# Plain float32 products for the first four steps of a fused attention and feed-forward kernel, with their operands split later

## The chip, the cores and the metric

The kernel runs on one core of one Trainium2 chip. The metric is the device time of one execution in microseconds (us), as the median of several runs. The core has five engines that run their own queues in order and wait for each other through semaphores: TensorE (PE, matrix products; PEld is its weight load), VectorE (DVE), ScalarE (ACT), GpSimd (POOL) and SyncE (SP, which issues the DMAs).

## The reference

```python
s_l = concat([scale * q_l @ k_g.T, where(|i-j| <= 32, scale * q_l @ k_l.T, -1e9)])   # per head
out_l = softmax(s_l) @ concat([v_g, v_l])        # 4 batches, 8 heads, 512 local rows, D = 64
out_g = softmax(scale * q_g @ concat([k_g, k_l]).T) @ concat([v_g, v_l])      # 32 global rows
x = concat([out_g, out_l])                       # 2176 tokens x 512
h = x @ w_in                                     # 512 -> 2048
y = where(h > 0, h, exp(min(h, 0)) - 1) @ w_out  # 2048 -> 512
yn = y / sqrt(mean(y * y) + 1e-6) * rms_g
out = (silu(yn @ w_gate) * (yn @ w_val)) @ w_o2  # 512 -> 1536 -> 512
```

The weights arrive as 64-bit floating-point numbers, and the kernel turns them into float32 on the chip.

## The kernel before

Local attention is done in 16 units (4 batches of 512 rows, 4 units of 128 rows each): `a_S` makes the scores on PE, `a_E` takes the maxima (DVE) and the exponentials (ACT), `a_T` transposes them (PE, copied by ACT), `a_PV` multiplies with V, and `a_N` divides by the sums (DVE) and writes x. The four units of the first batch are done in a start-up stretch. After it come four blocks of 16 steps (`moe_block`), one block for each batch. Step j of a block is `mm1` (12 products of 128x512 for one 128-column slice of the hidden layer), the activation `elu_a` (ACT and DVE), and `mm2` (12 products) of the step before, in two halves; in blocks 0 to 2 the attention units of the next batch stand between these (unit 4 with steps 0 to 2, unit 5 with steps 4 to 6, and so on; scores ahead of the first half of `mm2`, transposes between the halves).

Every operand of a product is kept in two parts, a rounded part of type fp32r and the remainder, and each product is three passes of these parts (`PASSES`, so 3 x 4 = 12 for each `mm1` and `mm2`). The parts are made by an ACT copy and a DVE subtraction: `split_hi` and `split_lo` for weights (L96, L99), `act1` for the activations (`g`, L139 and L140), `a_X` for x (`xT`, L289 and L290).

The weights of the first layer pair come in 16 pieces of 128x1024 (`order1`: two pieces of `w_in`, two of `w_out`, and again). Piece i is loaded as raw 64-bit words (L75), decoded by one ACT operation (L83) and four DVE operations (L90 to L93, `dec_bits`), and split (ACT L96, DVE L99). Pieces 0 to 2 are decoded and split in the start-up; in block 0 step j ends with `w1_decode` of piece j + 3, so that piece 15 goes with step 12. From step 13 on, `w2_task` decodes pieces of the second layer pair. Products of step j need the pieces of group j // 4: steps 0 to 3 use pieces 0 to 3 alone.

PE's order is written out by hand for the whole program, that of DVE and ACT for the start-up alone; elsewhere a scheduler at build time sets a fixed order for each queue, and each engine takes its queue in that order. Lines of the profile are those of this listing:

Of the kernel before, what the change touches and what calls it, by code (L numbers as in the profile page):

```python
# [21 lines left out]
P = 128  # L22
# [20 lines left out]
def fused_kernel(ctx: ExitStack, tc: tile.TileContext, kq, vl, gkq, gv, w_in, w_out, w_gate, w_val, w_o2, rms_g, consts, out):  # L43
# [44 lines left out]
    def dec_bits(x, raw):  # L88
        word = words(raw)
        nc.vector.tensor_scalar(out=x, in0=x, scalar1=HI_MIN, scalar2=HI_MAX, op0=ALU.max, op1=ALU.min)  # L90
# [28 lines left out]
    def elu_a(h, n):  # L119
# [4 lines left out]
        return e  # L124

# [60 lines left out]
    with ExitStack() as ls:  # L186
# [51 lines left out]
        def a_E(u):  # L238
# [30 lines left out]
        def a_N(u):  # L269
# [6 lines left out]
            for par in range(2):  # L276
                o = os_[par]
                nc.vector.tensor_scalar(out=st[:, par, :, 0:1], in0=o[:, :, 64:65], scalar1=1e-9, scalar2=None, op0=ALU.add)
                nc.vector.reciprocal(st[:, par, :, 1:2], st[:, par, :, 0:1])
                nc.vector.tensor_tensor(out=x[:, par], in0=o[:, :, 0:64], in1=st[:, par, :, 1:2].to_broadcast([P, 4, 64]), op=ALU.mult)  # L280

        def a_X(b, cs, xT, pools):

            for c in cs:
                pool, tag = pools[c]
                pt = pool.tile([P, 512], F32, tag=tag, name="xtp")
                for T in range(4):
                    nc.tensor.transpose(pt[:, T * P:(T + 1) * P], x_t[b][:, T, c * P:(c + 1) * P], ident)
                hi = nc.scalar.copy(xT[c][:, 0, :], pt)  # L289
                lo = nc.vector.tensor_tensor(out=xT[c][:, 1, :], in0=pt, in1=f(xT[c][:, 0, :]), op=ALU.subtract)  # L290
            return hi, lo
# [28 lines left out]
        def moe_block(b, slot, after=None):  # L320
            n, t0 = 512, b * 512
            xT, ys, prev = xT_t.pop(b), None, None
            for j in range(16):
                h = mm1(xT, j, n)
# [11 lines left out]
                if carry:  # L336
                    finish_block((2, 3))
                elif prev is not None:
# [15 lines left out]
        raws, n_raw, n_dec = {}, [0], [0]  # L354
# [14 lines left out]
        def w1_bits(i):  # L369
            dec_bits(dxs[i], raws.pop(i))  # L370

        def w1_hi(i):
# [7 lines left out]
            split_hi(dst, dxs[i])  # L380
            dsts[i] = dst

# [17 lines left out]
        with tc.manual_schedule(engines={mybir.EngineType.DVE, mybir.EngineType.Activation}):  # L400
# [10 lines left out]
            w1_abs(0)  # L411
            a_S(0, ATT2)
# [100 lines left out]
        def slot0(j, part, h):  # L513
            g = act1(h, 512, elu_a) if part == 0 else None
# [568 lines left out]
```

## Time and profile before

| | us |
|---|---|
| median of 3 runs (899.45 to 902.01) | 899.69 |
| the profiled execution | 899.1 |
| its span | 897.3 |
| PE busy in it | 864.9 (96%) |
| DVE busy in it | 588.0 (66%) |
| ACT busy in it | 475.8 (53%) |

The span runs from the first to the last instruction; 1.8 us of the profiled execution lie outside it. An engine's busy share is a mean over the whole span; a stretch of it can have another limit than the rest. In the rows, "idle" in brackets is time in which the engine did nothing just before a group, and behind the arrow stands what ended it. Starts are in us from the beginning of the span.

### The profile page before, as it was taken

The page shows a single profiled execution, that of the slowest core. Times are in us where ns is not written, and L with a number is a line of the kernel's source. Part 1 is how long each engine was busy: PE and PEld are TensorE (multiplying, and loading weights), DVE is VectorE, ACT ScalarE, POOL GpSimd, SP SyncE. Part 2 cuts the span into 40 slices and gives each one's busy share as a digit, 9 for nine tenths or more (in the row PEclk, how much of TensorE's full clock was granted, in tenths as well). Part 3 has the DMA queues.
Part 4 walks back from the last instruction along what each step waited for, and adds up shares of the span by engine and source line. Part 5 has one row for each costly group of instructions (what it writes and reads, how often), then busy time and mean ns, then how long its engine had stood idle before and what let it go on. Part 6 is the DMA issues. An engine that isn't in the chain of part 4 may idle for free.

```text
span 897.3 us, 16243 instructions
## 1 busy us (share of the span) xinstructions
PE 864.9 (96%) x6652; PEld 736.4 (82%) x6652; DVE 588.0 (66%) x983; ACT 475.8 (53%) x863; POOL 19.4 (2%) x22
## 2 busy tenths in 40 slices
PE   4789999999999999999999999999999999999997
PEld 3567877888888888677888899997999998899995
DVE  4899988777677764443488656885355776365642
ACT  4677664555564444333456655664455665355531
POOL 0000000000000000000110101000100000000000
PEclk8999999999999999999999999999999999999999
DMA  9786365966678742441405532233222232133200
GB/s 361 289 305 198 124 255 178 300 229 203 228 273 267 248 163 112 148 177 60 167 1 188 179 114 91 96 120 118 81 96 94 95 119 80 59 118 118 95 24 35
DMA packets 60225, 139.26 MB, mean 155 GB/s; under 512 B 4856, under 2 KB 30584, under 8 KB 57592
## 3 DMA queue, kind: packets, MB, share of 16 engines
q1 hardware_dynamic: 60152, 138.23, 44.7%
q8 instruction: 52, 0.85, 0.4%
q14 instruction: 21, 0.17, 0.1%
HBM read 115.15 MB, written 23.07 MB: 154 GB/s over the span
## 4 chain that ended last, share of the span: by engine, by line
PE 79%; DVE 11%; DMA 4%; ACT 3%; issue 1%; SPq 0%; POOL 0%; ACTq 0%
PE y L146 16%; PE A L739 15%; PE h L132 15%; PE o L745 15%; PE Q L739 11%; DMA kq<-in_kq 2%; DVE dx L93 2%; DVE dx L92 1%; PE s L234 1%; PE ptp L252 1%; DVE wA L99 1%; PE o L265 1%; PE hg L675 1%; DMA raw<-in_moe_w_out 1%; DVE dx L90 1%
## 5 line engine op out<-in xcount | busy, mean ns | idle before, releaser
L146 PE MATMUL y<-g,wA 128*128 128x512 f32 x768 | 197.3, 400 | 4.7 <-DVE g L140 4.1
L132 PE MATMUL h<-xT,wA 128*128 128x512 f32 x768 | 186.5, 391 | 1.7 <-DVE xT L290 1.7
L146 PEld LDWEIGHTS y<-g,wA 128*128 128x128 f32 x768 | 140.0, 189 | 40.2 <-DVE g L140 6.0
L132 PEld LDWEIGHTS h<-xT,wA 128*128 128x128 f32 x768 | 143.5, 188 | 32.7 <-DVE xT L290 2.4
L739 PE MATMUL A<-xc,wS 128*128 128x384 f32 (+1 forms) x864 | 155.9, 328 | 1.7 <-ACT t L931 0.9
L739 PEld LDWEIGHTS A<-xc,wS 128*128 128x128 f32 x864 | 145.0, 188 | 6.6 <-ACT t L931 1.3
L745 PE MATMUL o<-wB,p 128*128 128x512 f32 x612 | 147.3, 392 | 0.7 <-DVE p L750 0.3
L745 PEld LDWEIGHTS o<-wB,p 128*128 128x128 f32 x612 | 113.6, 188 | 24.7 <-DVE p L750 2.5
L739 PE MATMUL Q<-xc,wS 128*128 128x384 f32 (+1 forms) x648 | 115.3, 326 | 0.0
L739 PEld LDWEIGHTS Q<-xc,wS 128*128 128x128 f32 x648 | 107.8, 188 | 0.0
L595 DVE TENSOR_TENSOR wS<-wraw,wS 128x1024 fp32r<-128x1024 f32 x63 | 78.5, 1246 | 36.2 <-ACT wS L594 36.0
L754 DVE TENSOR_TENSOR t<-t,Q 128x384 f32<-128x384 f32 (+1 forms) x108 | 55.9, 528 | 37.2 <-PE Q L739 24.0
L594 ACT CAST wS<-wraw 128x1024 fp32r<-128x1024 f32 x63 | 65.9, 1050 | 19.6 <-PE Q L739 11.4
L121 ACT ACTIVATE e<-h 128x512 f32<-128x512 f32 x48 | 29.0, 605 | 69.8 <-PE h L132 69.7
L139 ACT CAST g<-e 128x512 fp32r<-128x512 f32 x64 | 39.8, 621 | 47.3 <-DVE e L123 30.8
L123 DVE SCALAR_TENSOR_TENSOR e<-e,h 128x512 f32<-128x512 f32 x48 | 32.5, 678 | 33.3 <-ACT e L122 33.3
L140 DVE TENSOR_TENSOR g<-e,g 128x512 fp32r<-128x512 f32 x64 | 43.8, 684 | 9.4 <-ACT g L139 9.1
L750 DVE TENSOR_TENSOR p<-p,p 128x384 fp32r<-128x384 f32 x36 | 20.0, 557 | 43.1 <-ACT p L749 43.1
L83 ACT ACTIVATE dx<-raw 128x1024 f32<-128x1024 f32 x34 | 39.2, 1157 | 15.9 <-DMA raw<-in_moe_w_gate 6.0
L90 DVE TENSOR_SCALAR dx<-dx 128x1024 f32<-128x1024 f32 x34 | 23.2, 688 | 33.7 <-ACT dx L83 33.7
L246 ACT ACTIVATE E<-s,mx 128x128 f32<-128x128 f32 x128 | 34.8, 385 | 17.2 <-DVE mx L244 17.2
L92 DVE SCALAR_TENSOR_TENSOR dx<-raw,dx 128x1024 int32<-128x1024 int32 x34 | 41.9, 1239 | 0.6
(173 smaller groups left out, 867.1 us busy)
## 6 DMA issues: line engine op xcount, KB each, us to landing
wraw<-wS SPq DMA_DIRECT2D x63, 512.0 KB, 3.2
raw<-in_moe_w_out SPq DMA_DIRECT2D x14, 1024.0 KB, 7.6
raw<-in_moe_w_in SPq DMA_DIRECT2D x8, 1024.0 KB, 6.0
raw<-in_moe_w_gate SPq DMA_DIRECT2D x6, 1024.0 KB, 6.6
raw<-in_moe_w_val SPq DMA_DIRECT2D x6, 1024.0 KB, 5.7
wS<-raw SPq DMA_DIRECT2D x48, 128.0 KB, 2.4
gvr<-in_gv SPq DMA_DIRECT2D x8, 640.0 KB, 4.7
wS<-dx SPq DMA_DIRECT2D x36, 128.0 KB, 2.1
```

Of the source, the lines that this page charges most:

```text
L83: ins = nc.scalar.activation(x, f(words(raw)[:, :, 1]), AF.Abs)
L92: nc.vector.scalar_tensor_tensor(out=i32(x), in0=word[:, :, 1], scalar=-0x40000000, in1=i32(x), op0=ALU.bitwise_and, op1=ALU.bitwise_or)
L132: nc.tensor.matmul(h[:, :n], W1[c, G][:, ws, o:o + P], xT[c][:, xs, :n], start=(k == 0), stop=(k == 11))
L139: nc.scalar.copy(g[:, 0, :n], e[:, :n])
L140: nc.vector.tensor_tensor(out=g[:, 1, :n], in0=e[:, :n], in1=f(g[:, 0, :n]), op=ALU.subtract)
L146: nc.tensor.matmul(ys[dc][:, :n], W2[j][:, ws, dc * P:(dc + 1) * P], g[:, gs, :n], start=(j == 0 and k == 0), stop=(j == 15 and k == 2))
L246: nc.scalar.activation(e[par][:, pr, :], ss[par][:, pr, :], AF.Exp, bias=mx[:, par, pr:pr + 1], scale=SCALE)
L594: nc.scalar.copy(t[:, :, 0, :], raw)
L595: nc.vector.tensor_tensor(out=t[:, :, 1, :], in0=raw, in1=f(t[:, :, 0, :]), op=ALU.subtract)
L739: nc.tensor.matmul(ps[:, :n], w[:, 2 * (q % 4) + c, ws, :], x[:, c, xs, :n], start=(first and c == 0 and z == 0), stop=(c == 1 and z == 2) ...
L745: nc.tensor.matmul(o, p[:, pp, t * P:(t + 1) * P], Wo[j][:, ww, :], start=(first and z == 0), stop=(last and z == 2))
L754: nc.vector.tensor_tensor(out=t, in0=t, in1=ps, op=ALU.add)
```

## The change

The products of steps 0 to 3 of block 0 (`plain1`, `plain2`) are made with plain float32 operands, one product instead of three passes: on whole weights (pieces 0 to 3, decoded and not split), on a whole x (`xf`, copied by DVE and ACT in `a_X0`) and on a whole activation (`elu_a` alone, no `g`). The parts that later blocks need are made later: those of x by `x_halves`, which stands with step 1, those of pieces 0 to 3 by `w1_turn` with steps 12 to 15. Piece 3 is decoded with step 0, and pieces 4 to 15 with steps 1 to 12 as before. In `a_E` one operation scales both maxima of a unit, and in `a_N` one reciprocal serves both.

```diff
-    def dec_bits(x, raw):
+    def dec_bits(x, raw, dst=None, parts=(0, 1)):
...
+    def dec_or(x, word, dst):
         nc.vector.scalar_tensor_tensor(out=i32(x), in0=word[:, :, 1], scalar=-0x40000000, in1=i32(x), op0=ALU.bitwise_and, op1=ALU.bitwise_or)
-        nc.vector.scalar_tensor_tensor(out=i32(x), in0=word[:, :, 0], scalar=29, in1=i32(x), op0=ALU.logical_shift_right, op1=ALU.bitwise_or)
+        n = 1024 // len(dst)
+        for k, o in enumerate(dst):
+            r = slice(k * n, (k + 1) * n)
+            nc.vector.scalar_tensor_tensor(out=i32(o), in0=word[:, r, 0], scalar=29, in1=i32(x)[:, r], op0=ALU.logical_shift_right, op1=ALU.bitwise_or)
...
+    def plain1(x, j):
+        h = hps.tile([P, 512], F32, tag="h", name="h")
+        o = j * P
+        for c in range(4):
+            nc.tensor.matmul(h, P1[c][:, o:o + P], x[:, c, :], start=(c == 0), stop=(c == 3))
+        return h
+
+    def plain2(ys, e, j, dcs):
+        for dc in dcs:
+            nc.tensor.matmul(ys[dc], P2[j][:, dc * P:(dc + 1) * P], e, start=(j == 0), stop=False)
...
             for par in range(2):
                 nc.vector.tensor_reduce(out=mx[:, par, :], in_=ss[par], axis=AX.X, op=ALU.max)
-                nc.vector.tensor_scalar(out=mx[:, par, :], in0=mx[:, par, :], scalar1=-SCALE, scalar2=None, op0=ALU.mult)
+            nc.vector.tensor_scalar(out=mx, in0=mx, scalar1=-SCALE, scalar2=None, op0=ALU.mult)
+            for par in range(2):
...
+                nc.vector.tensor_scalar(out=st[:, par, :, 0:1], in0=os_[par][:, :, 64:65], scalar1=1e-9, scalar2=None, op0=ALU.add)
+            nc.vector.reciprocal(st[:, :, :, 1:2], st[:, :, :, 0:1])
+            for par in range(2):
+                nc.vector.tensor_tensor(out=x[:, par], in0=os_[par][:, :, 0:64], in1=st[:, par, :, 1:2].to_broadcast([P, 4, 64]), op=ALU.mult)
...
+        def x_halves(xT, c, pt):
+            nc.scalar.copy(xT[c][:, 0, :], pt)
+            nc.vector.tensor_tensor(out=xT[c][:, 1, :], in0=pt, in1=f(xT[c][:, 0, :]), op=ALU.subtract)
...
+        def a_X0(xf, pools):
+            pts = [x_turn(0, c, *pools[c]) for c in range(4)]
+            for c in range(4):
+                if c % 2:
+                    last = nc.vector.tensor_copy(xf[:, c, :], pts[c])
+                else:
+                    last_a = nc.scalar.copy(xf[:, c, :], pts[c])
+            return last, last_a
...
-                h = mm1(xT, j, n)
+                plain = b == 0 and j < 4
+                h = plain1(xf, j) if plain else mm1(xT, j, n)
                 g = slot(j, 0, h)
...
+                elif prev is not None and b == 0 and j <= 4:
+                    plain2(ys, prev, j - 1, (0, 1))
                 elif prev is not None:
                     mm2(ys, prev, j - 1, n, (0, 1))
                 slot(j, 1, None)
...
+        def w1_turn(i):
+            kind, a, G = order1[i]
+            w1_new(i)
+            dst = dsts.pop(i)
+            n = 2 // len(plains[i])
+            for k, src in enumerate(plains.pop(i)):
+                d = dst[:, k * n:(k + 1) * n]
+                src = src.rearrange("p (a n) -> p a n", a=n)
+                nc.scalar.copy(d[:, :, 0, :], src)
+                nc.vector.tensor_tensor(out=d[:, :, 1, :], in0=src, in1=f(d[:, :, 0, :]), op=ALU.subtract)
...
             a_E(3)
-            w1_hi(1)
             a_PV(2, Y2)
+            w1_abs(2)
+            plain_new(2)
             a_N(2)
             a_T(3, 0, yps, "y0")
             a_T(3, 1, yps, "y1")
-            w1_lo(1)
-            w1_abs(2)
+            w1_bits(2, (0,))
             a_PV(3, Y2)
             a_N(3)
             xT_t = {0: new_xT()}
-            a_X(0, (0, 1), xT_t[0], ATT2[:2] + HB)
-            last = a_X(0, (2, 3), xT_t[0], ATT2[:2] + HB)
-            w1_bits(2)
-            w1_hi(2)
-            w1_lo(2)
+            xf = wpool.tile([P, 2112], F32, tag="w", name="xf")[:, :2048].rearrange("p (c n) -> p c n", c=4)
+            last = a_X0(xf, ATT2[:2] + HB)
+            w1_bits(2, (1,))
...
         def slot0(j, part, h):
-            g = act1(h, 512, elu_a) if part == 0 else None
+            g = (elu_a(h, 512) if j < 4 else act1(h, 512, elu_a)) if part == 0 else None
             att_slot(0, j, part)
+            if j == 1 and part == 2:
+                for c in range(4):
+                    x_halves(xT_t[0], c, xf[:, c, :])
+            if part == 2 and j > 11:
+                w1_turn(j - 12)
             if part == 2:
                 with tc.issue_after(last[0].ins), tc.issue_after(last[1].ins):
-                    w1_decode()
+                    w1_plain(3) if j == 0 else w1_decode()
```

What is left out: `dec_mag` holds the first two decoding operations as they were; `plain_new` gives pieces 0 to 2 room in the pool of the weights and piece 3 in a staging pool; the splits of pieces 0 and 1 are taken out of the start-up; the second half of `mm2` is chosen as the first.

The build gives each queue a new order. Three places follow. First the queue of DVE from the transposed x of batch 0 on, before (`xtp` is the transposed x in PSUM, `dx` a piece under decoding; 562 is piece 2, 737 piece 3; `e_667` the activation of step 0):

```order
L290 TENSOR_TENSOR xT0_605<-xtp_609,xT0_605 128x512
L290 TENSOR_TENSOR xT1_606<-xtp_616,xT1_606 128x512
L290 TENSOR_TENSOR xT2_607<-xtp_623,xT2_607 128x512
L290 TENSOR_TENSOR xT3_608<-xtp_630,xT3_608 128x512
L90 TENSOR_SCALAR dx_562<-dx_562 128x1024
L90 TENSOR_SCALAR dx_737<-dx_737 128x1024
L91 TENSOR_SCALAR dx_562<-dx_562 128x1024
L91 TENSOR_SCALAR dx_737<-dx_737 128x1024
L92 SCALAR_TENSOR_TENSOR dx_562<-raw_130,dx_562 128x1024
L92 SCALAR_TENSOR_TENSOR dx_737<-raw_132,dx_737 128x1024
L93 SCALAR_TENSOR_TENSOR dx_562<-raw_130,dx_562 128x1024
L123 SCALAR_TENSOR_TENSOR e_667<-e_667,h_654 128x512
```

and in the changed program (L325 is the copy of `a_X0`, L315 the subtraction of `x_halves`, L96 to L104 are the old L90 to L93; 530 is piece 2, 707 piece 3, 753 piece 4):

```order
L325 COPY xf_599<-xtp_605 128x512
L325 COPY xf_599<-xtp_615 128x512
L100 SCALAR_TENSOR_TENSOR dx_530<-raw_130,dx_530 128x1024
L315 TENSOR_TENSOR xT0_595<-xf_599,xT0_595 128x512
L96 TENSOR_SCALAR dx_707<-dx_707 128x1024
L104 SCALAR_TENSOR_TENSOR wP_532<-raw_130,dx_530 128x1024
L315 TENSOR_TENSOR xT1_596<-xf_599,xT1_596 128x512
L315 TENSOR_TENSOR xT2_597<-xf_599,xT2_597 128x512
L315 TENSOR_TENSOR xT3_598<-xf_599,xT3_598 128x512
L97 TENSOR_SCALAR dx_707<-dx_707 128x1024
L96 TENSOR_SCALAR dx_753<-dx_753 128x1024
L134 SCALAR_TENSOR_TENSOR e_641<-e_641,h_636 128x512
```

The four subtractions that make the parts of x stand ahead of the activation of step 0 in both, though the changed listing puts them with step 1. Second, the queue of DVE up to the second part of `g` of step 11, before (1496 is piece 14, 1596 piece 15; `g_1397` belongs to step 10, `g_1481` to step 11):

```order
L140 TENSOR_TENSOR g_1397<-e_1393,g_1397 128x512
L91 TENSOR_SCALAR dx_1496<-dx_1496 128x1024
L92 SCALAR_TENSOR_TENSOR dx_1496<-raw_1221,dx_1496 128x1024
L90 TENSOR_SCALAR dx_1596<-dx_1596 128x1024
L93 SCALAR_TENSOR_TENSOR dx_1496<-raw_1221,dx_1496 128x1024
L91 TENSOR_SCALAR dx_1596<-dx_1596 128x1024
L123 SCALAR_TENSOR_TENSOR e_1477<-e_1477,h_1464 128x512
L92 SCALAR_TENSOR_TENSOR dx_1596<-raw_1323,dx_1596 128x1024
L99 TENSOR_TENSOR wA_1502<-dx_1496,wA_1502 128x2x512
L140 TENSOR_TENSOR g_1481<-e_1477,g_1481 128x512
```

and in the changed program (L457 is the subtraction of `w1_turn`: 532 is piece 2, 709 and 710 are piece 3; 1568 and 1655 are the first two pieces of the second layer pair; L164 is the old L140, and `g_1389` belongs to step 11):

```order
L97 TENSOR_SCALAR dx_1568<-dx_1568 128x1024
L457 TENSOR_TENSOR wA_1652<-wP_532,wA_1652 128x2x512
L100 SCALAR_TENSOR_TENSOR dx_1568<-raw_1515,dx_1568 128x1024
L96 TENSOR_SCALAR dx_1655<-dx_1655 128x1024
L457 TENSOR_TENSOR wA_1729<-wP_709,wA_1729 128x512
L104 SCALAR_TENSOR_TENSOR dx_1568<-raw_1515,dx_1568 128x1024
L457 TENSOR_TENSOR wA_1729<-wP_710,wA_1729 128x512
L134 SCALAR_TENSOR_TENSOR e_1385<-e_1385,h_1372 128x512
L97 TENSOR_SCALAR dx_1655<-dx_1655 128x1024
L134 SCALAR_TENSOR_TENSOR e_1426<-e_1426,h_1413 128x512
L100 SCALAR_TENSOR_TENSOR dx_1655<-raw_1517,dx_1655 128x1024
L164 TENSOR_TENSOR g_1389<-e_1385,g_1389 128x512
```

Work that the listing has with steps 12 to 14 (all four `w1_turn`, a whole piece of the second layer pair and three operations of the next, and the activation of step 12) stands ahead of that `g`; before, none of it did. Third, the loads in the queue of SP after the start-up, before (`kq_` and `v_` are those of attention units; the load of `kq__731` waits for PE to be done with unit 4's scores):

```order
L75 DMA raw_134<-in_moe_w_in 128x2x512
L205 DMA kq__731<-in_kq 128x1408
L75 DMA raw_647<-in_moe_w_out 128x2x512
L75 DMA raw_645<-in_moe_w_in 128x2x512
L75 DMA raw_746<-in_moe_w_out 128x2x512
```

and in the changed program:

```order
L75 DMA raw_134<-in_moe_w_in 128x2x512
L75 DMA raw_627<-in_moe_w_in 128x2x512
L75 DMA raw_716<-in_moe_w_out 128x2x512
L75 DMA raw_629<-in_moe_w_out 128x2x512
L229 DMA kq__701<-in_kq 128x1408
```

Three pieces of weights have moved ahead of a load that waits for PE.

## Rows read from the trace of the kernel before

**Rows 1.** Busy time by stretch: stretch, length, busy us of PE, PEld, DVE, ACT, POOL, granted clock, DMA share, GB/s.

```profile
90.00:112.00 22.00, 22.00 (x185) 17.66 (x188) 22.00 (x31) 14.81 (x27) 0.00 (x0) 1.00 0.35 118
112.00:135.00 23.00, 22.69 (x222) 18.10 (x212) 18.32 (x30) 14.21 (x26) 0.00 (x0) 1.00 0.67 251
200.00:400.00 200.00, 200.00 (x1892) 158.22 (x1891) 125.53 (x251) 94.50 (x186) 0.00 (x0) 1.00 0.60 206
```

**Rows 2.** PE's instructions in order of time: start, length, line, operation, count, [idle before].

```profile
39.24 3.03 PE L132 MATMUL h<-xT,wA 128*128 128x512 f32 x12 [1.29 <-DVE xT L290]
...
47.26 0.50 PE L146 MATMUL y<-g,wA 128*128 128x512 f32 x1 [0.64 <-ACT g L139]
50.33 1.80 PE L146 MATMUL y<-g,wA 128*128 128x512 f32 x5 [2.56 <-DVE g L140]
...
66.37 2.81 PE L146 MATMUL y<-g,wA 128*128 128x512 f32 x11 [0.96 <-DVE g L140]
...
81.23 0.66 PE L252 MATMUL ptp<-ident,E 128*128 128x128 f32 x4 [0.38 <-ACT E L246]
...
126.25 2.81 PE L146 MATMUL y<-g,wA 128*128 128x512 f32 x11 [0.31 <-DVE g L140]
...
147.73 0.66 PE L288 MATMUL xtp<-ident,x 128*128 128x128 f32 x4 [0.21 <-DVE xT L290]
...
152.53 0.73 PE L132 MATMUL h<-xT,wA 128*128 128x512 f32 x2 [0.46 <-DVE xT L290]
```

**Rows 3.** DVE's groups from 37 to 126 us: line, operation, tiles, count, busy us, mean ns, idle before.

```profile
L92 DVE SCALAR_TENSOR_TENSOR dx<-raw,dx 128x1024 int32<-128x1024 int32 x14 | 16.9, 1225 | 0.1
L93 DVE SCALAR_TENSOR_TENSOR dx<-raw,dx 128x1024 int32<-128x1024 int32 x13 | 15.7, 1212 | 0.0
L99 DVE TENSOR_TENSOR wA<-dx,wA 128x1024 fp32r<-128x1024 f32 x13 | 15.7, 1212 | 0.1
L91 DVE TENSOR_SCALAR dx<-dx 128x1024 int32<-128x1024 int32 x14 | 9.4, 684 | 0.0
L90 DVE TENSOR_SCALAR dx<-dx 128x1024 f32<-128x1024 f32 x14 | 9.4, 682 | 1.9 <-ACT dx L83 1.9
L140 DVE TENSOR_TENSOR g<-e,g 128x512 fp32r<-128x512 f32 x12 | 8.2, 681 | 0.0
L123 DVE SCALAR_TENSOR_TENSOR e<-e,h 128x512 f32<-128x512 f32 x12 | 8.0, 671 | 0.0
...
L244 DVE TENSOR_SCALAR mx<-mx 128x4 f32<-128x4 f32 x6 | 0.9, 155 | 0.0
L279 DVE RECIPROCAL st<-st 128x4 f32<-128x4 f32 x6 | 0.8, 160 | 0.0
```

**Rows 4.** DVE's instructions in order of time, as in rows 2.

```profile
92.56 0.69 DVE L91 TENSOR_SCALAR dx<-dx 128x1024 int32<-128x1024 int32 x1
93.16 2.36 DVE L92 SCALAR_TENSOR_TENSOR dx<-raw,dx 128x1024 int32<-128x1024 int32 x2
95.43 0.68 DVE L123 SCALAR_TENSOR_TENSOR e<-e,h 128x512 f32<-128x512 f32 x1
96.03 2.35 DVE L93 SCALAR_TENSOR_TENSOR dx<-raw,dx 128x1024 int32<-128x1024 int32 x2
...
133.80 0.69 DVE L123 SCALAR_TENSOR_TENSOR e<-e,h 128x512 f32<-128x512 f32 x1 [2.78 <-ACT e L122]
```

**Rows 5.** The chain of waits in the start-up: start, length, what.

```profile
32.48 0.94 ACT wA L96
...
33.45 1.22 DVE wA L99
```

**Rows 6.** PE in order of time: the one plain float32 product, 384 columns wide.

```profile
449.74 0.81 PE L633 MATMUL ms<-acc,ones 128*128 128x384 f32 x2
```

**Rows 7.** Busy time by stretch around PE's pause in step 1, columns as in rows 1.

```profile
48.00:52.00 4.00, 1.68 (x6) 1.02 (x7) 4.00 (x7) 3.84 (x10) 0.00 (x0) 0.90 0.99 394
52.00:56.00 4.00, 4.00 (x17) 3.33 (x17) 3.47 (x6) 3.54 (x8) 0.00 (x0) 0.68 0.88 359
```

More of the change, by code (lines that the diff above doesn't have):

```diff
@@ L276, in a_N, with x_turn @@
             for par in range(2):
[L277 to L280, printed above, removed]
+                nc.vector.tensor_scalar(out=st[:, par, :, 0:1], in0=os_[par][:, :, 64:65], scalar1=1e-9, scalar2=None, op0=ALU.add)
+            nc.vector.reciprocal(st[:, :, :, 1:2], st[:, :, :, 0:1])
+            for par in range(2):
+                nc.vector.tensor_tensor(out=x[:, par], in0=os_[par][:, :, 0:64], in1=st[:, par, :, 1:2].to_broadcast([P, 4, 64]), op=ALU.mult)
+        def x_turn(b, c, pool, tag):
+            pt = pool.tile([P, 512], F32, tag=tag, name="xtp")
+            for T in range(4):
+                nc.tensor.transpose(pt[:, T * P:(T + 1) * P], x_t[b][:, T, c * P:(c + 1) * P], ident)
+            return pt
+        def x_halves(xT, c, pt):
+            nc.scalar.copy(xT[c][:, 0, :], pt)
+            nc.vector.tensor_tensor(out=xT[c][:, 1, :], in0=pt, in1=f(xT[c][:, 0, :]), op=ALU.subtract)
         def a_X(b, cs, xT, pools):
             for c in cs:
[L285 to L291, printed above, removed]
+                x_halves(xT, c, x_turn(b, c, *pools[c]))
+        def a_X0(xf, pools):
[6 more added lines that the diff above has]
+            return last, last_a
         ATT2 = [(aps, "att")] * 4
@@ L337, in moe_block @@
                     finish_block((2, 3))
+                elif prev is not None and b == 0 and j <= 4:
+                    plain2(ys, prev, j - 1, (2, 3))
                 elif prev is not None:
@@ L351, in fused_kernel @@
         nc.vector.memset(eps, 1e-6)
-        raws, n_raw, n_dec = {}, [0], [0]
+        raws, n_raw, n_dec = {}, [0], [4]
         def w1_load(n=1):
@@ L367, in w1_abs, with w1_bits, w1_new @@
             dxs[i] = dec_abs(dec["t"], raws[i])
-        def w1_bits(i):
-            dec_bits(dxs[i], raws.pop(i))
-        def w1_hi(i):
+        plains = {}
+        def w1_bits(i, parts=(0, 1)):
+            dec_bits(dxs[i], raws[i], plains.get(i), parts)
+            if 1 in parts:
+                del raws[i]
+        def w1_new(i):
             kind, a, G = order1[i]
@@ L379, in w1_hi, with plain_new, w1_plain @@
                     W2[a + k] = dst[:, k]
-            split_hi(dst, dxs[i])
             dsts[i] = dst
+        def plain_new(i):
+            kind, a, G = order1[i]
+            if i == 3:
+                plains[i] = [stg.tile([P, 512], F32, tag="stg", name="wP") for _ in range(2)]
+            else:
+                if i != 1:
+                    plains["at"] = wpool.tile([P, 2112], F32, tag="w", name="wP")
+                plains[i] = [plains["at"][:, i % 2 * 1024:i % 2 * 1024 + 1024]]
+                if i:
+                    del plains["at"]
+            for k in range(2):
+                src = plains[i][k] if i == 3 else plains[i][0][:, k * 512:(k + 1) * 512]
+                (P1 if kind == "1" else P2)[a + k] = src
+        def w1_plain(i):
+            w1_abs(i)
+            plain_new(i)
+            w1_bits(i)
+            w1_load()
+        def w1_turn(i):
+            kind, a, G = order1[i]
+            w1_new(i)
[6 more added lines that the diff above has]
+                nc.vector.tensor_tensor(out=d[:, :, 1, :], in0=src, in1=f(d[:, :, 0, :]), op=ALU.subtract)
+            for k in range(2):
+                del (P1 if kind == "1" else P2)[a + k]
+        def w1_hi(i):
+            w1_new(i)
+            split_hi(dsts[i], dxs[i])
         def w1_lo(i):
@@ L411, in fused_kernel @@
             w1_abs(0)
+            plain_new(0)
             a_S(0, ATT2)
```

11 lines of the change are left out of this document (8 added, 3 removed).

## The prediction

> **What bounds the kernel now.** I read the busy time by stretch first, because the shares of the whole span mix stages. From 200 to 400 us PE is busy without a break, and DVE and ACT have room: there the products set the pace, and whatever shift reaches that stage is carried to the end. In block 0 it is another picture. From 90 to 112 us both PE and DVE are busy all the time, and only from 112 to 135 us does DVE have some 4.7 us left [rows 1]. So in block 0 two engines run side by side at their limits, and one has to ask which of them the other waits for. PE's order of time says it: between the first product at 39.24 us and 126.25 us PE stands still five times, 0.64 + 2.56 + 0.96 + 0.38 + 0.31 = 4.85 us, four of them for `g` and most of that for its second part, the DVE subtraction [rows 2]. DVE in the same stretch has one idle sum worth a name, 1.9 us in which it waits for ACT's first decoding step [rows 3], and its first real pause comes at 133.80 us, 2.78 us long, when the last piece is decoded [rows 4]. So DVE's queue is the chain of block 0, and it holds PE at one late point: the last wait for `g`, that of step 11, which ends at 126.25 us [rows 2]. Behind it PE runs on; it loses 0.21 + 0.46 us at the end of the block, waiting for the parts of x [rows 2], and nothing in the long stretch after [rows 1].
>
> The question is therefore: how much DVE work stands in the queue ahead of that `g` of step 11, before and after?
>
> **The start-up.** The splits of piece 1 lie on the chain of waits, 0.94 us on ACT and 1.22 us on DVE [rows 5], and both go. But ACT's place is taken by `dec_abs` of piece 2, which now stands ahead of unit 3's transposed copies and is of the size of a 1024-column ACT step; so the products with V of unit 3 do not come earlier, and the join of the two reciprocals makes the first half of `a_N` wait for the second. I take the last x of batch 0 at the same time as before. Then two DVE copies take the place of the first two subtractions, at the same price, so DVE's chain starts where it did, at about 37.3 us. The bounds are 1.0 us earlier (the joined small operations and half of the split) and 0.5 us later (the wait just named).
>
> **DVE's work ahead of `g` of step 11.** Prices are distances between starts, since the end of one overlaps the next: two 1024-column operations with two operands take 95.43 - 93.16 = 2.27, so 1.135 us each; a 1024-column operation with one operand takes 93.16 - 92.56 = 0.60; a 512-column one 96.03 - 95.43 = 0.60 [rows 4]. Now the counts, before from the groups [rows 3], after from the changed order of the queue, from the first copy of x to that `g`:
>
> - Heavy operations (L92, L93, L99): before 14 + 13 + 13 = 40. After: 16 times the old L92, 15 times the old L93 (one of them in two halves), 12 splits of pieces 4 to 15 and 4 splits by `w1_turn`, 47 in all. The 7 more cost 7 x 1.135 = 7.95 us. They are there because the build has put the work of later steps ahead of this `g`: all four `w1_turn`, and a whole piece and more of the second layer pair.
> - Light 1024-column operations (L90, L91): 28 before, 30 after, +2 x 0.60 = 1.2 us.
> - 512-column operations: two copies more, one activation more (that of step 12), four subtractions of `g` fewer (steps 0 to 3 have none): -0.6 us. The four subtractions for x stand in both.
> - The joined operations: three scalings and three reciprocals fewer in units 4 to 6, busy 0.155 and 0.160 us each [rows 3], about half of it hidden behind a neighbour: -0.5 us.
>
> Sum: 7.95 + 1.2 - 0.6 - 0.5 = **+8.05 us**. DVE's waits for ACT I keep at 1.9 us; three pieces are now loaded ahead of a load that waits for PE, but in the trace it is ACT's queue that holds DVE there, not the loads. Bounds: 0 (all of it gone) and twice as much.
>
> **PE's work up to there.** A plain product of 512 columns is not in the trace; a plain one of 384 columns is, and takes two instructions and 0.81 us with its tail [rows 6]. One fp32r pass costs 3.03 - 2.81 = 0.22 us (12 passes against 11 [rows 2]), so the three passes that a plain product replaces cost 0.66 us. That is the lower bound, no loss at all; the upper one is 0.81 x 4/3 = 1.08 us, the whole row scaled to 512 columns, tail and all. No row is nearer to one end, since the tail overlaps the next product by a part that this row does not show; I take the middle, 0.87 us. Steps 0 to 3 have 32 such products: 32 x 0.21 = **+6.7 us** (0 to 13.4). This is hidden: PE's own work between 39.24 and 126.25 us is 87.0 - 4.85 = 82.2 us; with 6.7 more it ends at 39.2 + 88.9 = 128.1 us, while DVE releases the `g` at 126.25 + 8.05 = 134.3 us. Even at the upper bound PE would only just be late (134.8 us). The pauses of PE in steps 0 to 2 move with it: I expect it to stand still once for some 4 us in step 1, ahead of the transposes of unit 4, since DVE now makes the parts of x, the whole of piece 2's end and half of piece 3 ahead of that unit's maxima. That too is covered.
>
> **After it.** From the `g` of step 11 on PE is the chain again. The work that DVE did early is missing later: the `w2` pieces are done, so the 0.21 + 0.46 us at the end of the block should go. The `w1_turn` results are needed only in block 1, and lie there in time. So 8.05 - 0.67 = **+7.4 us**, carried to the end. The profiled execution took 899.1 us, 0.6 us below the median of 899.69 us; it would become 906.5, and the median **907.1 us**.
>
> **Rivals.** By 0.3% (2.7 us) I mean what a measurement of this kernel can tell from no change.
>
> *Forecast, chance 0.80:* DVE's queue holds the `g` of step 11. With the bounds, 7.4 - 1.0 - 1.9 = +4.5 to 7.4 + 0.5 + 1.9 = +9.8, so 904.2 to 909.5 us.
>
> *The clock falls once more, 0.12.* After PE's pause of 2.56 us before 50.33 us [rows 2] the granted clock was 0.90 of full speed in one stretch of 4 us and 0.68 in the next [rows 7], so 4 x 0.10 + 4 x 0.32 = 1.7 us of full-speed work were lost. In block 0 that is covered if it happens in step 1. But PE will now also stand still in steps 10 to 12, close to the point behind which nothing covers it. One more such fall there gives 907.1 + 1.7 = 908.8 us, and with the upper bounds 911. The Trainium skill, "TensorE: Matmul & The Clock Gate", section "Why this matters for your kernels", warns of exactly this, that an idle gap amid matmuls sends the clock back to half rate; the granted clock of 0.68 here agrees that it falls after a pause. By the rule alone this rival would be the likeliest; by the rows it is open, since the 0.96 us pause at 66.37 us has no such stretch that I have shown.
>
> *DVE does not bind, 0.05.* If the moved work fits into gaps, PE alone sets the pace: 82.2 + 6.7 from 39.2 gives 128.1 against 126.25, less 0.67 at the end: +1.2, so 900.9 us, no change. Against it: a queue in order, full from 37 to 130 us.
>
> *The start-up is what counts, 0.03, faster.* The 0.94 + 1.22 us of piece 1's split [rows 5] come off the chain, and five pauses of 4.85 us were the cost of `g` that four steps no longer make. Then PE starts at 37.1, and if half its pauses went unfilled by plain products at the lower bound (0.66), the time is 899.7 - 2.2 - 2.4 = 895.1 us. It decides only if the DVE work ahead of the `g` of step 11 grows by less than the 2 us or so that an earlier start gives; I count 8.
>
> **How the numbers follow.** The forecast and the clock rival are slower by over 0.3%: 0.92. No change 0.05, faster 0.03. The range takes the forecast's own lower bound, 904.2, rounded to 904, and the clock rival's 911 above; it leaves out the two small rivals and a part of the tails.
>
> **What would show it.** DVE busy without a break from 37 us to about 133 us; PE idle before the second part of a `g` near 118 and 133 us, a few us in all; the wait for the `g` of step 11 ending near 134 us instead of 126.25; the first products of block 1 some 7 us later than before; plain products at about 0.87 us each. It is wrong if PE has no wait for `g` past 100 us, if the DVE queue has idle time of several us ahead of that `g`, or if a plain product takes well over 1.08 us, when PE itself would be late.

## The result, and the profile after

The changed kernel took 911.38 us in the median of four runs (908.6 to 912.67), the kernel before 899.9 us (899.45 to 902.01) beside it. The ratio is 1.0114, with a 95% interval of 1.0093 to 1.0135; it is taken over all executions and is not that of the two medians, which is 1.0128. Differences in us below are those of medians, and they can be larger than the ratio gives (11.5 us here against 10.3). The ratio on the 899.69 us of the table ahead is 909.9 us. The direction and most of the size are as forecast (907.1 us); the median itself lies 0.4 us above the range's upper end.

| | before | after |
|---|---|---|
| the profiled execution, us | 899.1 | 908.6 |
| its span | 897.3 | 906.8 |
| PE busy | 864.9 | 872.7 |
| DVE busy | 588.0 | 585.7 |
| ACT busy | 475.8 | 474.6 |

The profiled execution of after is the fastest of its four; its mean granted clock is 0.993, that of the other three 0.988 to 0.990.

PE's order of time after the change; these rows answer to [rows 2]:

```profile
39.19 3.70 PE L143 MATMUL h<-xf,wP 128*128 128x512 f32 x8 [0.50 <-ACT xf L327]
...
52.87 0.66 PE L277 MATMUL ptp<-ident,E 128*128 128x128 f32 x4 [3.22 <-ACT E L271]
...
65.86 3.60 PE L143 MATMUL h<-xf,wP 128*128 128x512 f32 x8
69.29 3.60 PE L148 MATMUL y<-e,wP 128*128 128x512 f32 x8
...
120.67 3.85 PE L170 MATMUL y<-g,wA 128*128 128x512 f32 x11 [2.80 <-DVE g L164]
...
135.10 0.50 PE L170 MATMUL y<-g,wA 128*128 128x512 f32 x1 [0.44 <-ACT g L163]
137.05 2.83 PE L170 MATMUL y<-g,wA 128*128 128x512 f32 x11 [1.45 <-DVE g L164]
...
162.81 0.40 PE L252 MATMUL s<-masks,identr 128*32 128x256 bf16 x8
```

The first product starts when it did (39.19 against 39.24 us). PE stands still in step 1, then at the `g` of step 9 and at that of step 11, whose second part now comes at 137.05 us instead of 126.25 [rows 2]. The last row is the scores of the first unit in block 1, 162.81 us. In the trace of before the same row is:

```profile
153.19 0.40 PE L228 MATMUL s<-masks,identr 128*32 128x256 bf16 x8
```

That is 9.6 us earlier, and the span of after is 9.5 us longer, so all of this execution's loss has been made by then. Of the plain products, each printed as two instructions, four take 69.29 - 65.86 = 3.43 us, 0.857 us each, close to four fp32r passes at the prediction's 0.22 us.

DVE in order of time around those two `g`:

```profile
116.52 1.23 DVE L110 TENSOR_TENSOR wA<-dx,wA 128x1024 fp32r<-128x1024 f32 x1
117.65 1.23 DVE L104 SCALAR_TENSOR_TENSOR dx<-raw,dx 128x1024 int32<-128x1024 int32 x1
118.79 1.23 DVE L457 TENSOR_TENSOR wA<-wP,wA 128x1024 fp32r<-128x1024 f32 x1
119.92 0.69 DVE L164 TENSOR_TENSOR g<-e,g 128x512 fp32r<-128x512 f32 x1
...
134.57 0.69 DVE L134 SCALAR_TENSOR_TENSOR e<-e,h 128x512 f32<-128x512 f32 x1 [1.95 <-ACT e L133]
135.18 1.22 DVE L100 SCALAR_TENSOR_TENSOR dx<-raw,dx 128x1024 int32<-128x1024 int32 x1
136.31 0.69 DVE L164 TENSOR_TENSOR g<-e,g 128x512 fp32r<-128x512 f32 x1
```

Ahead of the first `g` stands a turn (L457) that block 1 needs; ahead of the second stand all four turns, the last of which the listing has with step 15, and the activation of step 12, for which DVE itself waits 1.95 us, because that activation's products are late.

Busy time by stretch, columns as in [rows 1]:

```profile
120.00:124.00 4.00, 3.33 (x11) 2.66 (x12) 4.00 (x9) 2.82 (x4) 0.00 (x0) 0.76 1.00 413
124.00:128.00 4.00, 4.00 (x16) 3.23 (x15) 4.00 (x7) 2.02 (x3) 0.00 (x0) 0.81 0.04 13
200.00:400.00 200.00, 200.00 (x1889) 159.63 (x1888) 127.93 (x234) 95.44 (x184) 0.00 (x0) 1.00 0.62 209
```

After PE's pause of 2.80 us the granted clock is 0.76 and 0.81 in two stretches, 4 x 0.24 + 4 x 0.19 = 1.7 us of full-speed work, close to the place behind which the forecast had nothing to cover it. From 200 to 400 us PE is busy without a break, as before [rows 1].

Two things had to be told apart then: what the plain products cost against what the joined small operations cost, and whether it is the amount of DVE's work or its place in the queue that costs.

### The profile page after: what moved, and what is told of

Same layout as the page of the kernel before. It is cut to its first block, busy times and chain, and to the rows that moved or that the text cites. A ratio compares the mean times of both kernels' runs of the same rounds, so it can differ in the third digit from the quotient of the medians.

```text
span 906.8 us, 16131 instructions
## 1 busy us (share of the span) xinstructions
PE 872.7 (96%) x6620; PEld 733.3 (81%) x6620; DVE 585.7 (65%) x951; ACT 474.6 (52%) x862; POOL 19.1 (2%) x22
## 4 chain that ended last, share of the span: by engine, by line
PE 81%; DVE 10%; DMA 3%; ACT 3%; issue 2%; POOL 0%; SPq 0%; ACTq 0%; DVEq 0%
PE y L170 16%; PE h L156 15%; PE A L824 15%; PE o L830 14%; PE Q L824 11%; DVE dx L100 2%; PE o L290 1%; PE ptp L277 1%; PE s L258 1%; DVE wA L110 1%; DVE dx L96 1%; PE hg L760 1%; DVE dx L104 1%; DMA raw<-in_moe_w_in 1%; PE xtp L310 1%
## 5 line engine op out<-in xcount | busy, mean ns | idle before, releaser
L170 PE MATMUL y<-g,wA 128*128 128x512 f32 x720 | 185.4, 401 | 5.2 <-DVE g L164 4.7
L156 PE MATMUL h<-xT,wA 128*128 128x512 f32 x720 | 175.9, 394 | 0.0
L170 PEld LDWEIGHTS y<-g,wA 128*128 128x128 f32 x720 | 131.5, 189 | 38.4 <-DVE g L164 6.5
L156 PEld LDWEIGHTS h<-xT,wA 128*128 128x128 f32 x720 | 135.3, 189 | 29.4 <-issue 1.0
L163 ACT CAST g<-e 128x512 fp32r<-128x512 f32 x60 | 37.3, 622 | 42.0 <-DVE e L134 24.8
L164 DVE TENSOR_TENSOR g<-e,g 128x512 fp32r<-128x512 f32 x60 | 41.0, 683 | 9.7 <-ACT g L163 9.2
L96 DVE TENSOR_SCALAR dx<-dx 128x1024 f32<-128x1024 f32 x34 | 23.4, 689 | 30.3 <-ACT dx L83 29.9
L100 DVE SCALAR_TENSOR_TENSOR dx<-raw,dx 128x1024 int32<-128x1024 int32 x34 | 41.9, 1234 | 0.6
```

Of the source, the lines that this page charges most:

```text
L156: nc.tensor.matmul(h[:, :n], W1[c, G][:, ws, o:o + P], xT[c][:, xs, :n], start=(k == 0), stop=(k == 11))
L163: nc.scalar.copy(g[:, 0, :n], e[:, :n])
L164: nc.vector.tensor_tensor(out=g[:, 1, :n], in0=e[:, :n], in1=f(g[:, 0, :n]), op=ALU.subtract)
L170: nc.tensor.matmul(ys[dc][:, :n], W2[j][:, ws, dc * P:(dc + 1) * P], g[:, gs, :n], start=(j == 0 and k == 0), stop=(j == 15 and k == 2))
```

## The experiments

Each was compared with the kernel before on the same chip. The changed kernel itself was not run again beside them, so a comparison with its 911.38 us goes over two sittings; the ratios are what to compare there. Each profile is of one execution, and its time is given where it stands well off the median.

**1. Turns and tasks of the second weights held behind `g`** (e1_hold, made from the changed kernel).

```diff
...
+                with tc.issue_after(g_ins[0].ins), tc.issue_after(g_ins[1].ins):
                     w1_turn(j - 12)
...
+                    with tc.issue_after(g_ins[0].ins), tc.issue_after(g_ins[1].ins):
                         w2_task()
```

> The changed kernel with one edit: in block 0 the four w1_turn and the first tasks of the second layer pair are tied behind the g of their own step (12 to 15) in the queues of DVE and ACT. All products stay as changed. Theory (DVE's queue holds the g of step 11 because the build put later steps' work ahead of it): the waits for g near 118 and 135 us fall below 0.7 us each, g of step 11 is released by about 131 us, PE's own work is the bound, and the time is 903 to 905 us. Rival (the cost is the plain products' own time on PE): the time stays within 2 us of the changed kernel's 911.4.

Measured 908.43 us, ratio 1.0096 (1.0077 to 1.0115), outside the ranges of both theory and rival; by the intervals the gain over the changed kernel is not clear of noise. PE of this kernel:

```profile
120.07 2.80 PE L172 MATMUL y<-g,wA 128*128 128x512 f32 x11 [0.76 <-DVE g L166]
...
158.63 0.40 PE L254 MATMUL s<-masks,identr 128*32 128x256 bf16 x8
...
188.45 0.40 PE L254 MATMUL s<-masks,identr 128*32 128x256 bf16 x8
```

The wait for `g` near 120 us fell from 2.80 to 0.76 us and that of step 11 went. In this profile the scores of block 1 began at 158.63 us instead of 162.81, although the kernel's first product was 1.5 us later, but the block then took 29.8 us to its next scores instead of 25.5. The theory held for the waits, the first of them 0.06 us above its 0.7; in this profile the whole gain was given back behind them (its span is 906.6 us, that of the changed kernel 906.8).

**2. The joins alone** (e3_joins, the kernel before with both joined operations, nothing else).

```diff
...
-                nc.vector.tensor_scalar(out=mx[:, par, :], in0=mx[:, par, :], scalar1=-SCALE, scalar2=None, op0=ALU.mult)
+            nc.vector.tensor_scalar(out=mx, in0=mx, scalar1=-SCALE, scalar2=None, op0=ALU.mult)
...
-                nc.vector.reciprocal(st[:, par, :, 1:2], st[:, par, :, 0:1])
...
+            nc.vector.reciprocal(st[:, :, :, 1:2], st[:, :, :, 0:1])
...
```

> The kernel before with the joined scaling and joined reciprocal alone. By the sum of the prediction these take about 0.5 us off DVE: 899 to 900 us. Rival (the build orders the queues anew, and the joined scaling waits for both maxima and then stands behind decoding operations, so the exponentials and the transposes come later): PE idle 1 to 2 us more ahead of the transposes of units 4 to 6, and 902 to 904 us.

Measured 905.17 us, ratio 1.0051 (1.0035 to 1.0067). This is the rival, and more than it: joining these small operations, six of them in block 0, costs 5.4 us (4.6 us by the ratio). DVE of this kernel at the maxima of unit 6:

```profile
105.28 1.28 DVE L243 TENSOR_REDUCE mx<-s 128x4 f32<-128x512 f32 x2
106.47 0.68 DVE L90 TENSOR_SCALAR dx<-dx 128x1024 f32<-128x1024 f32 x1
107.07 0.68 DVE L140 TENSOR_TENSOR g<-e,g 128x512 fp32r<-128x512 f32 x1
107.68 1.22 DVE L93 SCALAR_TENSOR_TENSOR dx<-raw,dx 128x1024 int32<-128x1024 int32 x1
108.81 0.16 DVE L244 TENSOR_SCALAR mx<-mx 128x8 f32<-128x8 f32 x1
```

and its PE:

```profile
111.07 0.66 PE L253 MATMUL ptp<-ident,E 128*128 128x128 f32 x4 [1.83 <-ACT E L247]
...
125.34 2.83 PE L146 MATMUL y<-g,wA 128*128 128x512 f32 x11 [1.53 <-DVE g L140]
```

Between the reductions and the scaling stand a part of `g` and two decoding operations of a weight. PE waits 1.83 us for exponentials, and later 1.53 us for the `g` of step 10. The trace of before has neither wait; its transposes of unit 6 start at once:

```profile
106.63 1.04 PE L252 MATMUL ptp<-ident,E 128*128 128x128 f32 x8
```

**3. PE's pauses filled** (e4_filler, the changed kernel with this added): 3 plain products in step 1, 12 single passes in step 10 and 5 in step 12, into the next step's accumulator, where they are overwritten.

```diff
...
+                if b == 0 and j in (10, 12,):
+                    fill(j + 1, {10: 12, 12: 5}[j], lambda t: nc.tensor.matmul(t, W1[0, 2][:, 0, 0:P], xT[0][:, 0, :], start=True, stop=True))
...
```

> The changed kernel with PE's pauses filled: 3 plain products before the transposes in step 1, 12 fp32r passes before the mm2 in step 10 and 5 before that in step 12, into the tile of the next h, which the next mm1 overwrites. DVE's and ACT's work is the same. Theory (beyond the DVE queue, 4 us of the 11.5 come from the clock, which falls after the pauses and lets the activation of step 12 come late): granted clock of the span 0.993 or more in all runs, no half-clock stretch between 115 and 130 us, and 906 to 908.5 us. Rival (the clock has no part, DVE alone sets the time): 910 us or more.

Measured 908.17 us, ratio 1.0088 (1.0073 to 1.0104). Its stretches:

```profile
120.00:124.00 4.00, 2.94 (x13) 2.11 (x12) 4.00 (x7) 3.47 (x4) 0.00 (x0) 1.00 0.98 398
124.00:128.00 4.00, 4.00 (x19) 3.32 (x18) 4.00 (x9) 2.33 (x4) 0.00 (x0) 1.00 0.23 95
```

Full clock where the changed kernel had 0.76 and 0.81. The mean clock of the six executions is 0.991 to 0.998, one of them below the theory's 0.993. The median is 911.38 - 908.17 = 3.2 us lower, the profiled execution 1.5 us (908.6 and 907.11), and the two intervals overlap. So filling the pauses did not slow the kernel, and the clock is worth perhaps 1.5 to 3 us of the loss; the size is not shown closer.

**4. Pieces 3 and 4 also held behind the scaled maxima of unit 4** (e5_hold_maxima, experiment 1 with this added).

```diff
...
-                    w1_plain(3) if j == 0 else w1_decode()
+                    if j == 0:
+                        with tc.issue_after(mx_ins[4].ins):
+                            w1_plain(3)
+                    elif j == 1:
+                        with tc.issue_after(mx_ins[4].ins):
+                            w1_decode()
...
```

> e1_hold with one more edit: in the queues of DVE, pieces 3 and 4 are tied behind the scaled maxima of unit 4. Theory (PE's pause of 3.2 us in step 1 is DVE decoding ahead of these maxima): the pause in step 1 falls below 0.7 us and the time is 3 us below e1_hold, 899.5 to 902 us. Rival (DVE's work is only moved, and PE waits later for the same time): the time is that of e1_hold within 1 us.

Measured 903.51 us, ratio 1.0041 (1.0028 to 1.0055), clear of experiment 1 but 1.5 us above the theory's upper end. The profiled execution took 906.48 us, 3 us above the median. In it the pause of step 1 is gone and the scores of block 1 begin at 154.8 us, but the block takes 31.5 us to its next scores. I put that down to the held tasks of the second weights, which keep raw buffers long.

**5. As 4, with those tasks left free** (e6_turns_held).

```diff
-                    with tc.issue_after(g_ins[0].ins), tc.issue_after(g_ins[1].ins):
-                        w2_task()
+                    w2_task()
```

> The changed kernel with the pieces 3 and 4 tied behind unit 4's scaled maxima and with the four turns of the first weight tied behind the split of g of their own step (12 to 15); the second weight's tasks are left free, unlike in e5_hold_maxima. Theory (VectorE's in-order queue at the waits for g and for the maxima is what costs, and e5 gave back 5 to 6 us in the second block only because its held second-weight tasks kept raw buffers until late): the waits for g near 118 and 135 us stay small as in e5 (below 1 us), the second block's scores to end go back from 31.6 us to about 25.5 to 27, and the time is 898 to 902 us, no more than 0.2% over the kernel before. Rival (what is freed at the front is lost again behind it whatever is held, because VectorE's and ScalarE's work there has only moved): 903 to 906, like e5, with the second block again at 29 us or more. Second rival (the second-weight tasks themselves stand in front of g): the wait near 135 us comes back to over 2 us and the time is 905 or more.

Measured 905.49 us, ratio 1.0058 (1.0037 to 1.0079), the first rival's range: my explanation fell, since block 1 still took 31.8 us. The profiled execution took 907.18 us, 1.7 us above the median. ACT in it shows what stood there:

```profile
173.69 1.12 ACT L83 ACTIVATE dx<-raw 128x1024 f32<-128x1024 f32 x1 [7.17 <-DMA raw<-in_moe_w_val]
174.72 0.58 ACT L132 ACTIVATE e<-h 128x512 f32<-128x512 f32 x1
```

and its PE what came of it:

```profile
177.63 0.80 PE L172 MATMUL y<-g,wA 128*128 128x512 f32 x1 [2.56 <-ACT g L165]
```

The stretches around it, columns as in [rows 1]:

```profile
176.00:180.00 4.00, 2.00 (x4) 1.31 (x5) 4.00 (x8) 1.75 (x3) 0.00 (x0) 0.63 0.37 157
180.00:184.00 4.00, 4.00 (x12) 3.09 (x11) 3.92 (x8) 0.62 (x1) 0.00 (x0) 0.52 0.66 197
```

In ACT's queue the first decoding step of a piece stands 7.17 us for its load, with the step's activation behind it; PE runs dry, and its clock falls. The trace of experiment 4 has the same row with a wait of 6.68 us, so the load explains that one too.

**6. The joined reciprocals alone** (e7_recip_only, the kernel before with this alone).

```diff
...
-                nc.vector.reciprocal(st[:, par, :, 1:2], st[:, par, :, 0:1])
...
+            nc.vector.reciprocal(st[:, :, :, 1:2], st[:, :, :, 0:1])
...
```

> The kernel before with the joined reciprocals only (one reciprocal of 8 values after both sums, the maxima scaled apart as before). e3_joins, with both joins, came to 905.17 against 899.8. Theory A (the joined scaling is what costs, because the first half's exponentials wait until both halves are reduced and scaled, 2.3 us behind the reduce in the trace of e3 against 1.2 before): this kernel stays at 899.0 to 900.5. Theory B (either join costs through the new order in which VectorE's queue is dealt, not through its own dependency): 902 to 905, with waits of TensorE for g or for exponentials in steps 8 to 12 that the kernel before has not.

Measured 905.6 us, ratio 1.0061 (1.0045 to 1.0077): 0.6 us above the range of theory B, and far from theory A. DVE of this kernel at unit 6:

```profile
107.44 1.28 DVE L243 TENSOR_REDUCE mx<-s 128x4 f32<-128x512 f32 x2
108.64 0.69 DVE L90 TENSOR_SCALAR dx<-dx 128x1024 f32<-128x1024 f32 x1
109.24 0.69 DVE L140 TENSOR_TENSOR g<-e,g 128x512 fp32r<-128x512 f32 x1
109.84 1.22 DVE L93 SCALAR_TENSOR_TENSOR dx<-raw,dx 128x1024 int32<-128x1024 int32 x1
110.97 0.24 DVE L244 TENSOR_SCALAR mx<-mx 128x4 f32<-128x4 f32 x2
```

and its PE:

```profile
113.23 0.66 PE L252 MATMUL ptp<-ident,E 128*128 128x128 f32 x4 [1.82 <-ACT E L246]
```

The scaling is not touched in this kernel, and yet it stands behind the same three operations as in experiment 2, with the same wait behind it (1.82 us). That wait is a part of the cost only: this trace also has 1.40 us ahead of the transposes of unit 5, where before had none, and a first product 1.6 us later than before's.

**7. The plain products without the joins** (e8_plain_only, the changed kernel with this undone).

```diff
-            nc.vector.tensor_scalar(out=mx, in0=mx, scalar1=-SCALE, scalar2=None, op0=ALU.mult)
+                nc.vector.tensor_scalar(out=mx[:, par, :], in0=mx[:, par, :], scalar1=-SCALE, scalar2=None, op0=ALU.mult)
...
-            nc.vector.reciprocal(st[:, :, :, 1:2], st[:, :, :, 0:1])
+                nc.vector.reciprocal(st[:, par, :, 1:2], st[:, par, :, 0:1])
```

> The changed kernel without the two joins: each half's maxima scaled and each half's sums inverted apart as in the kernel before, the plain float32 products and the moved parts kept. If the costs of the two halves of the change add up (11.5 in all, 5.4 of it by the joins alone in e3), this is 905.5 to 907 us. Rival (in the changed kernel the path is held by the parts made in steps 8 to 12 standing ahead of g, and the joins come beside that for nothing): 909 to 912. The forecast's own sum, with 0.5 us given to the joins, would have 907.6 against 907.1.

Measured 905.96 us, ratio 1.0064 (1.0046 to 1.0081). The two parts add up: 6.3 us here and 5.4 us in experiment 2, against 11.5 us for the whole change; by the ratios 0.64% and 0.51% against 1.14%. PE of this kernel:

```profile
113.62 0.66 PE L276 MATMUL ptp<-ident,E 128*128 128x128 f32 x4 [1.23 <-ACT E L270]
...
120.85 2.79 PE L170 MATMUL y<-g,wA 128*128 128x512 f32 x11 [0.98 <-DVE g L164]
...
134.61 2.83 PE L170 MATMUL y<-g,wA 128*128 128x512 f32 x11 [0.96 <-DVE g L164]
```

The `g` of step 11 comes at 134.61 us; the forecast had 134.3, or 134.8 without its 0.5 us for the joins. The granted clock stays at 1.00 from 116 to 128 us.

**8. The joins, with the decoding of steps 4 and 8 held behind the scaled maxima** (e9_joins_ordered, experiment 2 with this added).

```diff
...
-                    w1_decode()
+                    if j in (4, 8):
+                        with tc.issue_after(mx_ins[4 + j // 4].ins):
+                            w1_decode()
+                    else:
+                        w1_decode()
...
```

> e3_joins (the kernel before with both joins) with the decoding of steps 4 and 8 tied behind the scaled maxima of the unit of that step, so that the joined scaling does not stand behind decode rows in VectorE's queue. If e3's 5.4 us come from this place in the queue (scaling 2.3 us behind the reduces at 108.8 us, TensorE then 1.83 us without exponentials), this is 900 to 902. If the join's dependency itself costs (the first half's exponentials wait for the second half's maxima wherever the decoding stands), it stays at 904 to 906.

Measured 900.53 us, ratio 1.0009 (0.9997 to 1.0021). With the joins in place, an order that keeps the scaling ahead of that step's decoding gives back nearly all of the 5.4 us. DVE of this kernel at unit 6:

```profile
101.24 1.28 DVE L245 TENSOR_REDUCE mx<-s 128x4 f32<-128x512 f32 x2
102.44 0.69 DVE L90 TENSOR_SCALAR dx<-dx 128x1024 f32<-128x1024 f32 x1
103.03 0.69 DVE L140 TENSOR_TENSOR g<-e,g 128x512 fp32r<-128x512 f32 x1
103.64 0.17 DVE L246 TENSOR_SCALAR mx<-mx 128x8 f32<-128x8 f32 x1
```

One heavy operation (L93) no longer stands ahead of the scaling, and the unit's reductions themselves come 4 us earlier than in experiment 2 (1.4 us of it because the first product does). The joins' own dependencies are all still there, so it is the order that cost. What the same hold would do for the kernel before without the joins was not tried.

**9. Experiment 5 with two slots of block 1 left empty** (e10_slots; steps 1 and 2 take no task of the second weights; all tasks still run).

```diff
-                if part == 2 and j % 4 != 3:
+                if part == 2 and j % 4 != 3 and not (b == 1 and j in (1, 2)):
                     w2_task()
```

> e6_turns_held with the tasks of the second weights left out of the steps 1 and 2 of the second block (all 24 tasks still run, later). In e6 the front was mended (the second block's scores at 154.9 us, 1.7 after the kernel before), and 6.2 us were lost in that block (31.7 us to the next scores against 25.5): ScalarE's queue stood 7.17 us at the absolute value of a raw piece whose load landed at 173.7 us, with the step's activation behind it, and TensorE then waited 2.56 us and ran at half clock from 177.0 for 6.8 us. Theory (that one row stands in front of the activation because its step comes before its load can land): the second block takes 25.5 to 26.5 us again and the time is 898.5 to 901. Rival (the load is only one of several things that the later work meets there, or the work left out is missed later): 903 to 906.

Measured 901.76 us beside 900.58 of the kernel before, ratio 1.0012 (1.0001 to 1.0023): 0.8 us above the upper end of the theory's range, 1.2 us below the rival's. PE of this kernel:

```profile
115.35 2.79 PE L172 MATMUL y<-g,wA 128*128 128x512 f32 x11 [1.06 <-DVE g L166]
...
154.01 0.40 PE L254 MATMUL s<-masks,identr 128*32 128x256 bf16 x8
```

Block 1 begins 0.8 us after that of before and takes 25.6 us to its next scores (179.6 us). The changed kernel's operations are all there, joins and turns and plain products, and what is left of its 11.5 us is 1.2. So the changed kernel was slow by order, and by its amount of work by about that much at most.

**10. The kernel before with PE's pause in step 1 filled** by 11 passes (e11_before_fill), an attempt to beat it.

```diff
...
+                if b == 0 and j == 1:
+                    early[2] = hps.tile([P, 512], F32, tag="h", name="h")
+                    for _ in range(11):
+                        nc.tensor.matmul(early[2], W1[0, 0][:, 0, 0:P], xT[0][:, 0, :], start=True, stop=True)
```

> The kernel before with 11 more single pass products ahead of the first second-product rows of step 1, where TensorE pauses 0.64 and 2.56 us (46.6 to 50.3 us) and its clock is at half for 3.4 us from 51.2 on; their sums are overwritten by step 2's own. 11 products are 2.5 us of the 3.2 us of pauses. Theory (the clock falls because of that pause; half clock over 3.4 us costs 1.7 us): no half clock near 51 us, 897.8 to 899.0, that is, faster than the kernel before by 0.1 to 0.2%. Rival (the clock falls there for another reason, or the products delay the rows behind them by as much): 899.5 to 901.

Measured 899.57 us beside 900.58, ratio 0.9992 (0.9982 to 1.0003): perhaps faster by 0.1%, but the interval holds no change, and the time lies in the rival's range. Its stretch, which answers to the 0.68 of [rows 7]:

```profile
52.00:56.00 4.00, 3.45 (x19) 2.50 (x18) 3.96 (x7) 4.00 (x11) 0.00 (x0) 1.00 1.00 406
```

The clock stays up, so it was the pause that brought it down. At most 1.0 us of the 1.7 us came through; that DVE's queue, full in that stretch (3.96 of 4 us), covers the rest is the likely reason, but was not tried. No version tried here beats the kernel before by more than can be measured.

## Why the prediction was right, and where not

**DVE's queue as what binds block 0: right, and shown.** The `g` of step 11 came later because later steps' work stood ahead of it. Holding that work back shrank the waits at those `g` (experiments 1 and 9). DVE's groups from 37 us to the `g` of step 11 have the forecast's count:

```profile
L100 DVE SCALAR_TENSOR_TENSOR dx<-raw,dx 128x1024 int32<-128x1024 int32 x16 | 19.6, 1224 | 0.2
L104 DVE SCALAR_TENSOR_TENSOR dx<-raw,dx 128x1024 int32<-128x1024 int32 x13 | 15.8, 1219 | 0.1
L110 DVE TENSOR_TENSOR wA<-dx,wA 128x1024 fp32r<-128x1024 f32 x12 | 14.6, 1214 | 0.2 <-ACT wA L107 0.2
...
L134 DVE SCALAR_TENSOR_TENSOR e<-e,h 128x512 f32<-128x512 f32 x13 | 8.8, 679 | 2.0 <-ACT e L133 2.0
...
L457 DVE TENSOR_TENSOR wA<-wP,wA 128x1024 fp32r<-128x1024 f32 (+1 forms) x5 | 5.1, 1010 | 0.0
L104 DVE SCALAR_TENSOR_TENSOR wP<-raw,dx 128x512 int32<-128x512 int32 (+1 forms) x3 | 2.5, 862 | 0.0
```

In 1024-column operations these are 16 of L100, 13 + 2 of L104 (three rows of `wP`, two of them halves), 12 of L110 and 4 of L457 (five rows, two of them halves): 47.

**The joined operations, -0.5 us: wrong, and the step that failed.** The forecast priced them as six small operations fewer. Alone they cost 5.4 us (experiment 2), and taking them out of the changed kernel gives 911.38 - 905.96 = 5.4 us back (experiment 7; the two profiled executions are only 2.7 us apart). The reciprocals alone do it (experiment 6), through the new order in which the build deals DVE's queue, and an order set by hand undoes it (experiment 8). In the changed kernel I had read the order at the `g` of step 11, and not at the maxima. Of all terms this one was furthest off, and its sign was wrong.

**The sum of +8.05 us: right for the plain part, and the total in part by luck.** Without the joins the `g` of step 11 came at 134.61 us against 134.8 forecast for that case. With them it came at 137.05, 10.8 us later than before. Of the 2.75 us above the sum, 0.55 are a later first copy of x (37.85 against 37.3 us) and 1.3 more idle time of DVE ahead of that `g` (3.4 us instead of 2.1), which is the 1.95 us at the activation of step 12; the remaining 0.9 us are not traced to one row. In the time without the joins the forecast was 1.6 us too high (907.6 against 905.96), and for the joins it was 5.9 us too low (-0.5 against 5.4), so one error covers a part of the other.

**The clock rival, given 0.12: it came.** Its pause was the one that I expected near 118 us; the half clock behind it lay at 122 us and cost 1.7 us, as priced, in the profiled execution. They are not to be added to the 2.75 us: the late products that DVE waits for 1.95 us are those behind this pause and this half clock. The forecast itself named the pause and still held the fall for unlikely, since the 0.96 us pause of [rows 2] had no such stretch; but the new one was 2.80 us, nearer to the 2.56 us in front of [rows 7]. The Trainium skill, "TensorE: Matmul & The Clock Gate", section "Why this matters for your kernels", ties the drop to idle gaps amid matmuls; experiments 3 and 10 agree, the granted clock being 1.00 once the pause is filled. In the median the forecast stands 4.3 us low: 2.1 us of it in the profiled execution (908.6 against 906.5), the rest goes with runs at a mean clock lower by 0.003 to 0.005, which over 907 us is 2.7 to 4.5 us of full-speed work. That the clock makes the rest is not shown: in experiment 8 an execution with a mean clock of 0.988 took 899.97 us and one with 0.994 took 903.1.

**Plain products: right.** 0.857 us against 0.87, and covered. In experiment 9, where the order is mended, PE has them all and the kernel loses 1.2 us in the end: PE's longest pause in block 0 is 1.06 us, and it keeps its clock.

**The start-up at nothing, and the 0.67 us at the end of block 0: right.** The first product starts within 0.05 us, and PE no longer waits for the parts of x at the end of the block; DVE's first copy was 0.55 us late, at the bound of 0.5. The first product of other profiles lay up to 1.7 us later (40.9 us in experiment 2), by 1.5 us even where the start-up's code is the same (experiment 1 against the changed kernel), so a part of any single profile's difference lies in the start-up.

**The pause of 4 us in step 1: right in place and size,** 3.22 + 0.37 us, but not covered as forecast: holding two pieces behind the maxima, which takes it away, brought 4.9 us (908.43 to 903.51). How much of this is the pause, how much the clock behind it and how much the new order was not taken apart.

## What to carry to other kernels

Where a scheduler deals out in-order queues, cost an edit by the order that it produces at every place where a bottleneck engine is waited for, also where the edit only takes small operations away: here two joins cost 5.4 us, and the reciprocals alone about as much. Work that is due later has to be tied behind the result that is due now; but what is held must still come before its own due time, and what it displaces must not stand at a load that cannot have landed. A pause of PE can cost twice, once itself and once by the clock behind it (0.76 and 0.81 granted after the 2.80 us here), so a pause that is to move must be looked at for what covers its new place.

## What was not expected of the hardware

That more PE work need not make a kernel slower: 20 products in its pauses took the changed kernel from 911.38 to 908.17 us, a gain at the edge of the noise, with the granted clock at 1.00 instead of 0.76 and 0.81. And that ACT, busy for about half of the span, can stand 7.17 us at a load with urgent work behind it in its queue, and that this reaches PE as a wait of 2.56 us and a granted clock of 0.63 and 0.52 in the two stretches behind it.
